# Head dimension first for q and k, contiguous blocks for v and the weights, in a fused attention and mixture kernel

## The chip, the cores and the metric

The kernel runs on one core of one Trainium2 chip. The metric is device time in microseconds (us) of one execution; what the host does to the arrays before the launch is not in it.

## What is computed

A sliding-window attention with sink columns feeds a three-way maximum layer, and that feeds a routed layer of eight experts with a fixed capacity.

```python
scores = (q @ k.T) / sqrt(64)                 # batch 4, heads 8, 768 positions, head dimension 64
keep   = (pos_k < 4) | (0 <= pos_q - pos_k < 128)
a      = softmax(where(keep, scores, -1e9))
x      = (a @ v)                              # to [3072 tokens, 512]
h      = maximum(maximum(x @ w1, x @ w2), x @ w3)       # 512 -> 768
x2     = h @ w_out                            # 768 -> 512
# each token goes to one of 8 experts, 384 each, by the order of all logits x2 @ w_gate
out[t] = relu(x2[t] @ u1[e]) @ u2[e]          # 512 -> 1024 -> 512
```

## The kernel before

**Units and groups.** Attention is cut into 32 units. A unit is one batch, one half of the sequence (`hf`, 384 query rows) and one pair of heads `p`; it reads `nb` = 3 or 4 blocks of 128 key rows. Four units make a group of 384 tokens, and there are 8 groups. A unit goes through `load`, `prep`, `score`, `soft` and `pv`. The first 8 units are "native": their score matmuls take q and k as plain f32. The other 24 split each operand into a high fp32r part and a remainder, and multiply the parts.

**load and prep.** `load` fetches k, q and v with the sequence on the partitions, in rows of 256 B, one DMA for each head (L72, L73, L76), and the sink rows (L74, L77). `prep` (L79) turns them: TensorE transposes each 128x128 block of k and q through `flip` (L25) into the PSUM bank `pt`, of which pool `pst` has one. ScalarE copies out of it, for a native unit into `KZ` and `QF` (L89, L94 for the four sink columns that stand behind each block, L105), for the others into `KH` and `QS` (L89, L94, L114). For these VectorE subtracts to get the remainders (L90, L95, L115), with one operand in PSUM and one in SBUF, and ScalarE copies the high part of k to the other 64 partitions (L118). The unused half of each `KZ` is zero (L56). The native units have two sets of `KZ` in turn (`kf`, in memory lent by `Spare`, which shows as tiles `woh` and `wol`); `early` holds the first k and q loads there too.

**Weights of the first layer.** `single` (L239) loads one 512 KB piece of w1, w2, w3 (rows of 1 KB) or w_out (rows of 4 KB), as float64 words, into `st`, of which there are two buffers, and makes f32 of it on VectorE, ScalarE and GpSimd (L247 to L250). The second L250 of a piece frees its buffer for the next load. `split` makes high and low parts (L237, L238). `group` (L277) is then 216 matmuls of 384 columns for each group (L295), and `x2` 108 more (L317).

**Experts.** For each expert, `weights` (L541) loads 8 pairs `sa` (from u1, rows of 512 B) and `sb` (from u2, rows of 2 KB), two buffers each, splits them on ScalarE, GpSimd and VectorE (L549, L551), and TensorE runs L604 and L597. Between experts VectorE and TensorE choose the next tokens (`Route`).

**What sets the order.** `order` and `order1` (L620) give the order in which units and weight pieces are issued; a scheduler with its own time model then places the instructions on each engine. Each engine and the DMA queue of SyncE (SP) run in that order, so an instruction that waits holds up what is behind it. Tiles in a pool with one buffer (`kn`, `qn`, `vn`) are loaded again when their last reader is done.

Of the kernel before, what the change touches and what calls it, by code (L numbers as in the profile page):

```python
# [22 lines left out]
def f32(ap): return ap.bitcast(FT)  # L23
def flip(nc,out,x,ident):
    nc.tensor.transpose(out,x,f32(ident))  # L25

class Attn:
    def __init__(s, tc, q,k,v, keep, consts, pst, psp, pss, psv, work):
        s.tc=tc; s.nc=nc=tc.nc; s.q,s.k,s.v=q,k,v
# [14 lines left out]
        s.vn=consts.tile([16,2,64],FT,name="vns"); nc.vector.memset(s.vn,0.0)  # L44
# [3 lines left out]
        s.ks=consts.tile([128,2,64],FT,name="kss"); nc.vector.memset(s.ks,0.0)  # L48
# [3 lines left out]
        s.n=0; s.no=('kh0','kh1'); s.early=[]  # L52
# [10 lines left out]
    def load(s,b,hf,p,native=False):  # L63
        nc=s.nc; w=s.w
        nb=3+hf; S=768; D=64
        u=dict(b=b,hf=hf,p=p,nb=nb,n=s.n,nat=native); s.n+=1
        for x,c in (('kn',4),('qn',3)): u[x]=s.early.pop(0) if s.early else w.tile([128,c,2,64],FT,name=x,bufs=1)
        u['vn']=w.tile([128,4,2,64],FT,name="vnn",tag="vsp") if u['nat'] else w.tile([128,4,2,64],FT,name="vn",bufs=1)
        t0=hf*384; tk=t0-128*hf
        def rows(x,h,t,n): return bass.AP(tensor=x.tensor,offset=x.offset+((b*8+2*p+h)*S+t)*D,ap=[[D,128],[128*D,n],[1,D]])  # L70
# [3 lines left out]
        if hf: nc.sync.dma_start(s.ks[0:4],bass.AP(tensor=s.k.tensor,offset=s.k.offset+(b*8+2*p)*S*D,ap=[[D,4],[S*D,2],[1,D]]))  # L74
        for h in range(2):
            nc.sync.dma_start(u['vn'][:,:nb,h,:],rows(s.v,h,tk,nb))  # L76
            nc.sync.dma_start(s.vn[8*h:8*h+8,h],bass.AP(tensor=s.v.tensor,offset=s.v.offset+(b*8+2*p+h)*S*D,ap=[[0,2],[D,4],[1,D]]))  # L77
        return u
    def prep(s,u):  # L79
        nc=s.nc; w=s.w; nb=u['nb']; nat=u['nat']  # L80
        pk=s.pst.tile([128,512],FT,name="pt")
        for c in range(nb):
            flip(nc,pk[:,c*128:(c+1)*128],u['kn'][:,c].rearrange("p h d -> p (h d)"),s.ident)
        def pkv(a): return pk[a,:nb*128].rearrange("p (c j) -> p c j",j=128)
        half=[(slice(64*h,64*h+64),slice(64-64*h,128-64*h)) for h in range(2)]
        KZ=s.kf[u['n']%len(s.kf)] if nat else s.kz[u['n']%len(s.kz)]
        if not nat: KH=[s.two(u,[128,4,132],FR,f"kh{h}") for h in range(2)]
        for h,(a,o) in enumerate(half):
            nc.scalar.activation((KZ if nat else KH)[h][a,:nb,0:128],pkv(a),AF.Copy)  # L89
            if not nat: nc.vector.tensor_tensor(KZ[h][a,:nb,0:128],pkv(a),f32(KH[h][a,:nb,0:128]),op=OP.subtract)  # L90
        def sinks(src):
            for h,(a,o) in enumerate(half):
                ks=src[a][:,None,:].to_broadcast([64,nb-1,4])
                nc.scalar.activation((KZ if nat else KH)[h][a,:nb-1,128:132],ks,AF.Copy)  # L94
                if not nat: nc.vector.tensor_tensor(KZ[h][a,:nb-1,128:132],ks,f32(KH[h][a,:nb-1,128:132]),op=OP.subtract)  # L95
# [4 lines left out]
        if u['hf']:  # L100
            flip(nc,pq[:,384:512],s.ks.rearrange("p h d -> p (h d)"),s.ident)
            sinks(pq[:,384:388])
        if nat:
            QF=w.tile([128,384],FT,name="qf",tag="qs0",bufs=2)
            nc.scalar.activation(QF,pq[:,:384],AF.Copy)  # L105
            u.update(KZ=KZ,QF=QF)
# [62 lines left out]
    def pv(s,u,x):  # L169
# [6 lines left out]
        psk=s.psp.tile([128,512],FT,name="pp")  # L176
# [51 lines left out]
class Moe1:  # L228
    def __init__(s, tc, w1,w2,w3,wout,wgate, consts, wpool, main, conv, mm, pt, pss, ident):
        s.tc=tc; s.nc=tc.nc; s.mm=mm; s.pss=pss; s.main=main; s.conv=conv; s.ident=ident; s.consts=consts  # L230
        s.src=(w1,w2,w3); s.wout=wout; s.wgate=wgate
# [7 lines left out]
    def single(s,src):  # L239
# [506 lines left out]
```

## Time and profile before

| | us |
|---|---|
| three runs: lowest, median, highest | 1033.73, 1038.49, 1040.44 |
| the profiled execution: its own time | 1031.47 |
| its span, first to last instruction | 1029.7 |
| TensorE (PE) busy | 964.8 (94%) |
| VectorE (DVE) busy | 756.8 (73%) |
| ScalarE (ACT) busy | 511.5 (50%) |
| GpSimd (POOL) busy | 409.2 (40%) |

PE busy time counts the pipelined tail of each matmul, so a matmul of 384 columns shows some 340 ns although the next one starts after some 174. The profiled execution was 7.0 us faster than the median of the three runs. It falls into an opening of 100 us, in which attention of the first units and the weights of the first layer are made ready, a long middle to about 625 us with the other units under the matmuls of `group` and `x2`, and the experts.

### The profile page before, as it was taken

The page shows a single profiled execution, that of the slowest core. Times are in us where ns is not written, and L with a number is a line of the kernel's source. Part 1 is how long each engine was busy: PE and PEld are TensorE (multiplying, and loading weights), DVE is VectorE, ACT ScalarE, POOL GpSimd, SP SyncE. Part 2 cuts the span into 40 slices and gives each one's busy share as a digit, 9 for nine tenths or more (in the row PEclk, how much of TensorE's full clock was granted, in tenths as well). Part 3 has the DMA queues.
Part 4 walks back from the last instruction along what each step waited for, and adds up shares of the span by engine and source line. Part 5 has one row for each costly group of instructions (what it writes and reads, how often), then busy time and mean ns, then how long its engine had stood idle before and what let it go on. Part 6 is the DMA issues. An engine that isn't in the chain of part 4 may idle for free.

```text
span 1029.7 us, 19074 instructions
## 1 busy us (share of the span) xinstructions
PE 964.8 (94%) x6857; PEld 878.4 (85%) x6857; DVE 756.8 (73%) x1866; ACT 511.5 (50%) x1166; POOL 409.2 (40%) x355
## 2 busy tenths in 40 slices
PE   5989999999999999999999999898999988999996
PEld 3668889989999999999999998777777877888896
DVE  6799876787988888899886444878888868843330
ACT  5865553676666676665764311332433333344431
POOL 3766636244443434454343100324334243363431
PEclk9899999999999999999999999998999999999999
DMA  6654512132121121121210000424244253464430
GB/s 147 173 150 123 158 43 67 54 98 54 36 57 48 40 78 39 37 66 42 57 42 1 1 1 18 148 88 144 93 134 144 83 165 113 132 197 123 154 102 32
DMA packets 148846, 89.63 MB, mean 87 GB/s; under 512 B 90160, under 2 KB 133680, under 8 KB 148752
## 3 DMA queue, kind: packets, MB, share of 16 engines
q1 hardware_dynamic: 144048, 74.39, 26.0%
q0 software_dynamic: 3840, 12.45, 3.6%
q10 hardware_dynamic: 864, 1.57, 0.4%
q8 instruction: 54, 0.88, 0.3%
q14 instruction: 40, 0.33, 0.1%
HBM read 74.76 MB, written 13.76 MB: 86 GB/s over the span
## 4 chain that ended last, share of the span: by engine, by line
PE 54%; DVE 25%; issue 6%; DMA 6%; ACT 5%; POOL 2%; SPq 0%; POOLq 0%; DVEq 0%; ACTq 0%
PE mm L295 22%; PE mm L604 7%; PE acc L597 7%; PE mm L317 4%; PE po L206 2%; DMA sa<-in_moe_w_dram 2%; PE pt L25 2%; DMA st<-in_moe_w_dram 2%; PE rc L404 2%; DVE th L398 2%; DVE cA L250 2%; DVE A_w L188 1%; PE pp L25 1%; PE ps L142 1%; DVE hl L608 1%
## 5 line engine op out<-in xcount | busy, mean ns | idle before, releaser
L551 POOL TENSOR_TENSOR wal<-sa,wah 128x512 fp32r<-128x512 f32 x64 | 87.4, 1366 | 196.5 <-ACT wah L549 187.0
L202 POOL TENSOR_TENSOR L<-A_w,H 128x768 fp32r<-128x768 f32 x46 | 87.1, 1894 | 141.0 <-ACT H L201 121.8
L317 PE MATMUL mm<-woh,hh 128*128 128x260 f32 (+1 forms) x288 | 84.1, 295 | 2.5 <-DVE LG L320 1.1
L317 PE MATMUL mm<-woh,hl 128*128 128x260 f32 (+1 forms) x288 | 82.8, 292 | 1.9 <-DVE hl L303 1.2
L549 ACT ACTIVATE wah<-sa 128x512 fp32r<-128x512 f32 x64 | 40.4, 631 | 84.4 <-PE mm L604 44.5
L317 PE MATMUL mm<-wol,hh 128*128 128x260 f32 (+1 forms) x288 | 82.3, 287 | 0.0
L298 DVE TENSOR_TENSOR hm<-mm,hm 128x384 f32<-128x384 f32 x96 | 53.0, 552 | 37.6 <-PE mm L295 36.5
L597 PE MATMUL acc<-wbh,hl 128*128 128x512 f32 x192 | 78.5, 409 | 0.2 <-DVE hl L608 0.2
L597 PE MATMUL acc<-wbl,hh 128*128 128x512 f32 x192 | 78.5, 409 | 0.0
L597 PE MATMUL acc<-wbh,hh 128*128 128x512 f32 x192 | 78.2, 407 | 0.0
L549 ACT ACTIVATE wbh<-sb 128x512 fp32r<-128x512 f32 x64 | 40.3, 630 | 75.4 <-PE acc L597 66.5
L608 DVE SCALAR_TENSOR_TENSOR hl<-mm,hh 128x384 fp32r<-128x384 f32 x64 | 35.4, 553 | 56.3 <-ACT hh L607 56.0
L295 PE MATMUL mm<-xh,w0h 128*128 128x384 f32 x192 | 67.3, 351 | 2.0 <-ACT xh L284 1.1
L551 DVE TENSOR_TENSOR wbl<-sb,wbh 128x512 fp32r<-128x512 f32 x64 | 45.6, 714 | 31.5 <-ACT wbh L549 31.0
L295 PE MATMUL mm<-xh,w1h 128*128 128x384 f32 x192 | 66.6, 347 | 2.1 <-DVE hm L298 1.3
L295 PE MATMUL mm<-xl,w0h 128*128 128x384 f32 x192 | 65.6, 342 | 0.8 <-DVE xl L285 0.8
L295 PE MATMUL mm<-xh,w2h 128*128 128x384 f32 x192 | 66.0, 344 | 0.2 <-ACT hm L297 0.2
L295 PE MATMUL mm<-xh,w2l 128*128 128x384 f32 x192 | 65.2, 339 | 0.0
L295 PE MATMUL mm<-xh,w1l 128*128 128x384 f32 x192 | 65.0, 339 | 0.0
L295 PE MATMUL mm<-xl,w2h 128*128 128x384 f32 x192 | 64.8, 338 | 0.0
L295 PE MATMUL mm<-xl,w1h 128*128 128x384 f32 x192 | 64.8, 337 | 0.0
L295 PE MATMUL mm<-xh,w0l 128*128 128x384 f32 x192 | 64.7, 337 | 0.0
(334 smaller groups left out, 3113.4 us busy)
## 6 DMA issues: line engine op xcount, KB each, us to landing
sa<-in_moe_w_dram SPq DMA_DIRECT2D x64, 256.0 KB
sb<-in_moe_w_dram SPq DMA_DIRECT2D x64, 256.0 KB
st<-in_moe_w_dram SPq DMA_DIRECT2D x18, 512.0 KB
qn<-in_q_dram SPq DMA_DIRECT2D x60, 96.0 KB
x2d<-xo SPq DMA_DIRECT2D x18, 256.0 KB
kn<-in_k_dram SPq DMA_DIRECT2D x32, 128.0 KB
st<-in_moe_w_out_dram SPq DMA_DIRECT2D x6, 512.0 KB
vn<-in_v_dram SPq DMA_DIRECT2D x24, 128.0 KB
```

The source lines that it names most:

```text
L25: nc.tensor.transpose(out,x,f32(ident))
L202: nc.gpsimd.tensor_tensor(L,Af,f32(H),op=OP.subtract)
L206: nc.tensor.matmul(po[:,q:q+n],u['VS'][:,blk,128*h:128*h+128],part[:,c:c+n],start=(part is H and j==0),stop=False,skip_group_check=True)
L250: nc.vector.scalar_tensor_tensor(A,st[:,:,1],-0x40000000,A,op0=OP.bitwise_and,op1=OP.bitwise_or)
L295: nc.tensor.matmul(ps[:,:384],s.W[i][a][:,p,f*128:(f+1)*128],X[p][b],start=(n==0),stop=(n==11)); n+=1
L298: else: nc.vector.tensor_tensor(m,ps[:,:384],m,op=OP.max)
L317: nc.tensor.matmul(ps[:,:n],H[f][a][:,t*128:(t+1)*128],s.WO[b][:,f,u,:n],start=(k==0),stop=(k==17)); k+=1
L549: nc.scalar.activation(h,src,AF.Copy)
L551: (nc.vector if s.cv%2==0 else nc.gpsimd).tensor_tensor(l,src,f32(h),op=OP.subtract)
L597: nc.tensor.matmul(acc[t],H[f][a][:,t*128:(t+1)*128],W[f][1][b],start=(f==0 and n==0),stop=(f==F-1 and n==2)); n+=1
L604: nc.tensor.matmul(ps[:,:384],W[f][0][a][:,k,:],X[k][b],start=(n==0),stop=(n==11)); n+=1
L608: nc.vector.scalar_tensor_tensor(l,ps[:,:384],0.0,f32(h),op0=OP.max,op1=OP.subtract)
```

## The change

The host lays the arrays out before the launch. q comes as [128, 384] for each unit: two heads times 64 along the partitions, query rows along the free axis. k comes the same way, with the four sink columns stored behind each block of 128 (132 columns in all). v comes as [128, up to 512], the sink rows of v as one small array `vs`, the words of w1, w2, w3 and w_out as 24 pieces of [128, 4 KB], and u1 in rows of 2 KB. All transposes of k and q go. A native unit's k is loaded right into its half of `KZ`, of which there are now three sets, and its q into `QF`. For the others the ScalarE copies and the VectorE subtractions read `kn` and `qn` in SBUF. `zeros` clears only the unused half of a tile. The transposes of the sink weights in `pv` write to `pst` in place of `psp`.

```diff
     def zeros(s,ts):
-        for t in ts: s.nc.vector.memset(f32(t) if t.dtype==FR else t,0.0)
+        for h,t in enumerate(ts): s.nc.vector.memset((f32(t) if t.dtype==FR else t)[64-64*h:128-64*h],0.0)
...
-        for h in range(2):
-            nc.sync.dma_start(u['kn'][:,:nb,h,:],rows(s.k,h,tk,nb))
-            nc.sync.dma_start(u['qn'][:,:3,h,:],rows(s.q,h,t0,3))
...
+        if native:
+            u['KZ']=s.kf[u['n']%len(s.kf)]
+            for h,(a,o) in enumerate(half): nc.sync.dma_start(u['KZ'][h][a,:nb],turned(h,a))
+            u['QF']=w.tile([128,384],FT,name="qf",tag="qs0",bufs=2)
+            nc.sync.dma_start(u['QF'],s.q[i])
+            u['vn']=w.tile([128,4,2,64],FT,name="vnn",tag="vsp")
+        else:
+            u['kn']=w.tile([128,4,132],FT,name="kn",bufs=1)
+            nc.sync.dma_start(u['kn'][:,:nb],s.k[i].rearrange("h d (c j) -> (h d) c j",j=132)[:,:nb])
+            u['qn']=w.tile([128,384],FT,name="qn",bufs=1)
+            nc.sync.dma_start(u['qn'],s.q[i])
+            u['vn']=w.tile([128,4,2,64],FT,name="vn",bufs=1)
+        nc.sync.dma_start(u['vn'][:,:nb],s.v[i].rearrange("t (c h d) -> t c h d",h=2,d=64)[:,:nb])
+        u['sv']=w.tile([16,2,64],FT,name="vns")
+        nc.sync.dma_start(u['sv'],s.vs[b*4+p].rearrange("r (h d) -> r h d",h=2))
...
-        for c in range(nb):
-            flip(nc,pk[:,c*128:(c+1)*128],u['kn'][:,c].rearrange("p h d -> p (h d)"),s.ident)
...
-            nc.scalar.activation((KZ if nat else KH)[h][a,:nb,0:128],pkv(a),AF.Copy)
-            if not nat: nc.vector.tensor_tensor(KZ[h][a,:nb,0:128],pkv(a),f32(KH[h][a,:nb,0:128]),op=OP.subtract)
...
-        for c in range(3):
-            flip(nc,pq[:,c*128:(c+1)*128],u['qn'][:,c].rearrange("p h d -> p (h d)"),s.ident)
...
             for h,(a,o) in enumerate(half):
-                nc.scalar.activation(QS[h][a,:],pq[a,:384],AF.Copy)
-                nc.vector.tensor_tensor(QS[h][o,:],pq[a,:384],f32(QS[h][a,:]),op=OP.subtract)
-
-                fl=nb*132-4
-                nc.scalar.activation(KH[h][o].rearrange("p c j -> p (c j)")[:,:fl],f32(KH[h][a].rearrange("p c j -> p (c j)")[:,:fl]),AF.Copy)
+                k=flat(u['kn'])[a]
+                for r in (a,o): nc.scalar.activation(flat(KH[h])[r],k,AF.Copy)
+                nc.vector.tensor_tensor(flat(KZ[h])[a],k,f32(flat(KH[h])[a]),op=OP.subtract)
+                nc.scalar.activation(QS[h][a,:],u['qn'][a],AF.Copy)
+                nc.vector.tensor_tensor(QS[h][o,:],u['qn'][a],f32(QS[h][a,:]),op=OP.subtract)
...
-        psk=s.psp.tile([128,512],FT,name="pp")
+        psk=s.pst.tile([128,512],FT,name="pt")
...
-            A.kf=[A.zeros([A.extra.tile([128,4,132],FT,tag=f'kf{i}{h}') for h in range(2)]) for i in range(2)]
-            A.early=[A.extra.tile([128,4,2,64],FT,tag=f'e{i}') for i in range(4)]
+            A.kf=[A.zeros([A.extra.tile([128,4,132],FT,tag=f'kf{i}{h}') for h in range(2)]) for i in range(3)]
...
-        nc.sync.dma_start(a,s.w1[bass.ds(ev,1)].rearrange("a (k p) n -> p (a k) n",p=128)[:,:,f*128:(f+1)*128])
+        nc.sync.dma_start(a,s.w1[bass.ds(ev,1)].rearrange("a (f p) (k n) -> (a f) p k n",p=128,k=4)[f])
...
+def layout(np, i):
...
+    q, k, v = (np.asarray(i[n]).reshape(4, 4, 2, 768, 64) for n in 'qkv')
+    qt = q.transpose(0, 1, 2, 4, 3).reshape(4, 4, 128, 2, 384).transpose(0, 3, 1, 2, 4)
...
+        kt[:, hf, :, :, :, :nb, :128] = k[:, :, :, t].transpose(0, 1, 2, 4, 3).reshape(4, 4, 2, 64, nb, 128)
+        kt[:, hf, :, :, :, :nb, 128:] = k[:, :, :, :4].transpose(0, 1, 2, 4, 3)[:, :, :, :, None, :]
...
+    u1 = np.asarray(i['moe2_w1']).reshape(8, 4, 128, 8, 128).transpose(0, 3, 2, 1, 4)
```

In the changed kernel the lines have moved: L70, L72, L76, L78, L80 and L82 load k (native), q (native), k, q, v and the sinks of v; L99 to L102 are the copies and subtractions of `prep`; L123 are the native score matmuls, L227 the loads of `st`, L276 the matmuls of `group`.

On PE the program begins like this before (`ps<-woh,qf` is a score matmul of a native unit, `pt<-ident` a transpose of its k or q):

```order
L25 MATMUL pt<-ident,woh 128x128 x3
L25 MATMUL pt<-ident,wol 128x128 x3
L139 MATMUL ps<-woh,qf 128x132 x2
L139 MATMUL ps<-woh,qf 128x260
L25 MATMUL pt<-ident,wol 128x128 x3
L139 MATMUL ps<-woh,qf 128x260 x3
L25 MATMUL pt<-ident,wol 128x128 x3
```

and like this with the change, where the score matmuls stand first:

```order
L123 MATMUL ps<-woh,qf 128x132 x2
L123 MATMUL ps<-woh,qf 128x260 x4
L123 MATMUL ps<-woh,qf 128x132 x2
L123 MATMUL ps<-woh,qf 128x260 x4
L123 MATMUL ps<-woh,qf 128x132
L123 MATMUL ps<-wol,qf 128x132
L123 MATMUL ps<-woh,qf 128x260
L123 MATMUL ps<-wol,qf 128x260
```

The transposes ahead of each unit's scores are gone, and three units' scores stand in a row.

On the DMA queue of SP in the opening, before (`kn` and `qn` are loads for the transposes, `vnn` is v, `st` a weight piece):

```order
L263 DMA wg<-in_moe_w_gate_dram 128x4x8
L72 DMA kn<-in_k_dram 128x4x64 x2
L245 DMA st<-in_moe_w_dram 128x4x256
L73 DMA qn<-in_q_dram 128x3x64 x2
L245 DMA st<-in_moe_w_dram 128x4x256
L72 DMA kn<-in_k_dram 128x4x64 x2
L73 DMA qn<-in_q_dram 128x3x64 x2
L74 DMA kss<-in_k_dram 4x2x64
L77 DMA vns<-in_v_dram 8x1x64 x2
L245 DMA st<-in_moe_w_dram 128x4x256
L76 DMA vnn<-in_v_dram 128x3x64 x2
```

and with the change at the same place, where k goes straight into the tiles `woh` and `wol` that the score matmuls of an earlier unit read:

```order
L244 DMA wg<-in_wg_dram 128x4x8
L70 DMA woh<-in_k_dram 64x528
L72 DMA qf<-in_q_dram 128x384
L227 DMA st<-in_words_dram 128x1024
L70 DMA wol<-in_k_dram 64x528
L76 DMA kn<-in_k_dram 128x396
L227 DMA st<-in_words_dram 128x1024
L80 DMA vnn<-in_v_dram 128x384
L227 DMA st<-in_words_dram 128x1024
L70 DMA woh<-in_k_dram 64x528
L72 DMA qf<-in_q_dram 128x384
L70 DMA woh<-in_k_dram 64x528
```

Fewer DMAs are left, and weight pieces now stand behind loads of k and q into tiles that score matmuls release.

On DVE in the middle, around the remainders of one unit with four blocks, before (`kz<-pt,kh` reads PSUM and SBUF):

```order
L90 TENSOR_TENSOR kz_113<-pt,kh_w 64x4x128
L151 COPY_PREDICATED T_w<-ca,ps 128x128
L153 COPY_PREDICATED T_w<-ca,negs 128x8
L175 TENSOR_TENSOR psn<-T_w,psn 128x6x4
L90 TENSOR_TENSOR kz_114<-pt,kh_w 64x4x128
L151 COPY_PREDICATED T_w<-ca,ps 128x128 x2
L157 TENSOR_REDUCE m<-T_w 128x6
L209 TENSOR_TENSOR x_3855<-po,x_3855 64x384
L298 TENSOR_TENSOR hm<-mm,hm 128x384
L163 TENSOR_TENSOR T_w<-T_w,m 128x792
L95 TENSOR_TENSOR kz_113<-pt,kh_w 64x3x4
L298 TENSOR_TENSOR hm<-mm,hm 128x384
```

and with the change, where `kz<-kn,kh` and `qs<-qn,qs` read SBUF twice:

```order
L100 TENSOR_TENSOR kz_109<-kn,kh_w 64x528
L172 TENSOR_TENSOR A_w<-pp,ul 128x768
L135 COPY_PREDICATED T_w<-ca,ps 128x128
L150 TENSOR_SCALAR l<-l 128x6
L102 TENSOR_TENSOR qs_4274<-qn,qs_4274 64x384
L284 TENSOR_TENSOR hl_3178<-hm,hh_3177 128x384
L130 COPY_PREDICATED T_w<-ca,ps 128x128
L131 COPY_PREDICATED T_w<-ca,ps 128x4
L151 RECIPROCAL l<-l 128x6
L100 TENSOR_TENSOR kz_110<-kn,kh_w 64x528
L135 COPY_PREDICATED T_w<-ca,ps 128x128
L102 TENSOR_TENSOR qs_4275<-qn,qs_4275 64x384
```

The two small sink subtractions are gone, and those of k and q stay, with another source.

## Rows read from the trace of the kernel before

**Rows 1.** Busy time of each engine by stretch: from:to in us, length, then each engine.

```profile
0.00:100.00 100.00, 82.28 (x423) 63.24 (x424) 84.65 (x180) 65.72 (x189) 59.75 (x62) 0.97 0.57 151
100.00:150.00 50.00, 47.47 (x290) 41.79 (x291) 42.51 (x82) 29.35 (x68) 24.61 (x23) 1.00 0.36 104
150.00:600.00 450.00, 440.55 (x3032) 430.81 (x3031) 362.32 (x759) 271.04 (x629) 182.01 (x156) 1.00 0.18 47
650.00:900.00 250.00, 224.97 (x2055) 189.37 (x2054) 204.13 (x692) 87.80 (x171) 93.61 (x73) 0.97 0.40 125
```

**Rows 2.** Chain that ended last, 0 to 150 us: start, length, what.

```profile
3.75 0.51 DVE woh L56
4.29 0.89 PE pt L25 x3
5.20 0.48 ACT woh L89
...
6.63 0.91 PE pt L25 x3
7.57 0.50 ACT qf L105
8.11 2.11 PE ps L139 x6
...
83.86 3.76 DMA st<-in_moe_w_dram
...
147.53 0.33 PE pt L25 x3
```

**Rows 3.** The same chain's later pieces, 150 us to the end.

```profile
175.94 3.72 DMA st<-in_moe_w_out_dram
...
751.11 4.65 DMA sa<-in_moe_w_dram
...
827.84 7.53 DMA sa<-in_moe_w_dram
```

**Rows 4.** Who waited for whom on DVE, 0 to 50 us: total, times, longest.

```profile
DVE T_w L151 <- ACT T_w L150: 5.1, 5, 1.7
DVE T_w L146 <- PE ps L139: 3.1, 1, 3.1
```

**Rows 5.** Transposes by tile kn, qn, kss in 150 to 600 us: PE, then PEld.

```profile
150.00:600.00 450.00, 12.30 (x75) 9.36 (x75) 1.00 0.18 47
150.00:600.00 450.00, 10.50 (x63) 7.88 (x63) 1.00 0.18 47
150.00:600.00 450.00, 3.27 (x12) 1.69 (x12) 0.00 (x0) 1.00 0.18 47
```

**Rows 6.** VectorE by line: shortest, median, longest ns. L115, L298 read PSUM; L303 SBUF twice.

```profile
L115 DVE TENSOR_TENSOR qs<-pt,qs x48: 550/555/560, 86.8 to 539.4; 64x384 fp32r<-64x384 f32 x48
L298 DVE TENSOR_TENSOR hm<-mm,hm x96: 536/557/562, 72.9 to 623.8; 128x384 f32<-128x384 f32 x96
L303 DVE TENSOR_TENSOR hl<-hm,hh x48: 516/558/2101, 81.1 to 625.0; 128x384 fp32r<-128x384 f32 x48
```

**Rows 7.** Groups by form: count, then busy us and mean ns of one.

```profile
L303 DVE TENSOR_TENSOR hl<-hm,hh 128x384 fp32r<-128x384 f32 x48 | 36.0, 750 | 7.7 <-ACT hh L302 7.3
L298 DVE TENSOR_TENSOR hm<-mm,hm 128x384 f32<-128x384 f32 x96 | 53.0, 552 | 37.6 <-PE mm L295 36.5
```

**Rows 8.** The removed ScalarE copies and VectorE sink subtractions, by line: shortest, median, longest ns.

```profile
L89 ACT ACTIVATE woh<-pt x16: 483/534/595, 5.2 to 58.9; 64x384 f32<-64x384 f32 x8, 64x512 f32<-64x512 f32 x8
L94 ACT ACTIVATE woh<-pt x16: 158/172/176, 6.2 to 61.9; 64x8 f32<-64x8 f32 x8, 64x12 f32<-64x12 f32 x8
L105 ACT ACTIVATE qf<-pt x8: 472/490/490, 7.6 to 62.1; 128x384 f32<-128x384 f32 x8
L95 DVE TENSOR_TENSOR kz<-pt,kh_w x26: 114/164/177, 75.3 to 517.0; 64x8 fp32r<-64x8 f32 x14, 64x12 fp32r<-64x12 f32 x12
```

**Rows 9.** What the SP queue waited for: total, times, longest.

```profile
SPq L72 <- PE ps L143: 67.1, 13, 10.4
SPq L72 <- PE pt L25: 52.2, 11, 10.9
```

More of the change, by code (lines that the diff above doesn't have):

```diff
@@ L27, with __init__ @@
 class Attn:
-    def __init__(s, tc, q,k,v, keep, consts, pst, psp, pss, psv, work):
-        s.tc=tc; s.nc=nc=tc.nc; s.q,s.k,s.v=q,k,v
+    def __init__(s, tc, q,k,v,vs, keep, consts, pst, psp, pss, psv, work):
+        s.tc=tc; s.nc=nc=tc.nc; s.q,s.k,s.v,s.vs=q,k,v,vs
         s.pst,s.psp,s.pss,s.psv,s.w=pst,psp,pss,psv,work
@@ L43, in __init__ @@
         s.ps=consts.tile([128,160],FR,name="psn"); nc.vector.memset(f32(s.ps),0.0)
-        s.vn=consts.tile([16,2,64],FT,name="vns"); nc.vector.memset(s.vn,0.0)
         s.vk=[]
@@ L47, in __init__ @@
             t=consts.tile([128,2,128],FR,name=f"vk{i}"); nc.vector.memset(f32(t),0.0); s.vk.append(t)
-        s.ks=consts.tile([128,2,64],FT,name="kss"); nc.vector.memset(s.ks,0.0)
         s.kf=[]; s.kz=[s.zeros([consts.tile([128,4,132],FR,name=f"kz{h}") for h in range(2)])]
@@ L51, in __init__ @@
         nc.scalar.activation(t,t,AF.Exp)
-        s.n=0; s.no=('kh0','kh1'); s.early=[]
+        s.n=0; s.no=('kh0','kh1')
         s.extra=None
@@ L66, in load, with turned @@
         u=dict(b=b,hf=hf,p=p,nb=nb,n=s.n,nat=native); s.n+=1
[L67 to L70, printed above, removed]
-        for h in range(2):
-            nc.sync.dma_start(u['kn'][:,:nb,h,:],rows(s.k,h,tk,nb))
-            nc.sync.dma_start(u['qn'][:,:3,h,:],rows(s.q,h,t0,3))
[L74 to L77, printed above, removed]
+        i=(b*2+hf)*4+p; c=nb*132; half=[(slice(64*h,64*h+64),slice(64-64*h,128-64*h)) for h in range(2)]
+        def turned(h,a): return s.k[i,h].rearrange("d (c j) -> d c j",j=132)[:,:nb]
+        if native:
[13 more added lines that the diff above has]
+        nc.sync.dma_start(u['sv'],s.vs[b*4+p].rearrange("r (h d) -> r h d",h=2))
         return u
@@ L80, in prep @@
         nc=s.nc; w=s.w; nb=u['nb']; nat=u['nat']
-        pk=s.pst.tile([128,512],FT,name="pt")
-        for c in range(nb):
-            flip(nc,pk[:,c*128:(c+1)*128],u['kn'][:,c].rearrange("p h d -> p (h d)"),s.ident)
-        def pkv(a): return pk[a,:nb*128].rearrange("p (c j) -> p c j",j=128)
         half=[(slice(64*h,64*h+64),slice(64-64*h,128-64*h)) for h in range(2)]
-        KZ=s.kf[u['n']%len(s.kf)] if nat else s.kz[u['n']%len(s.kz)]
-        if not nat: KH=[s.two(u,[128,4,132],FR,f"kh{h}") for h in range(2)]
@@ L88, in prep @@
-        for h,(a,o) in enumerate(half):
-            nc.scalar.activation((KZ if nat else KH)[h][a,:nb,0:128],pkv(a),AF.Copy)
-            if not nat: nc.vector.tensor_tensor(KZ[h][a,:nb,0:128],pkv(a),f32(KH[h][a,:nb,0:128]),op=OP.subtract)
[L91 to L95, printed above, removed]
@@ L96, in prep @@
-        if not u['hf']: sinks(pk[:,0:4])
-        pq=s.pst.tile([128,512],FT,name="pt")
-        for c in range(3):
-            flip(nc,pq[:,c*128:(c+1)*128],u['qn'][:,c].rearrange("p h d -> p (h d)"),s.ident)
[L100 to L106, printed above, removed]
@@ L107, in prep @@
         VK=u['VK']=s.vk[u['n']%2]
         hi,lo=(bass.AP(tensor=VK.tensor,offset=VK.offset+o,ap=[[VK.ap[0][0],16],[st,2],[1,64]]) for o,st in (((0,64),(128,64)) if nat else ((0,192),(64,64))))
-        nc.gpsimd.tensor_copy(hi,s.vn)
-        nc.gpsimd.tensor_tensor(lo,s.vn,f32(hi),op=OP.subtract)
+        nc.gpsimd.tensor_copy(hi,u['sv'])
+        nc.gpsimd.tensor_tensor(lo,u['sv'],f32(hi),op=OP.subtract)
         if not nat:
+            KZ=s.kz[u['n']%len(s.kz)]
+            KH=[s.two(u,[128,4,132],FR,f"kh{h}") for h in range(2)]
@@ L618, in expert, with attention_mixtures @@
             s.scat.append(st)
-def attention_mixtures(tc,q,k,v,w1,w2,w3,wo,wg,u1,u2,out,off=236,native=8,order='a0 a0 a0 a0 w a1 a1 w w w w w a1 a1 a2',order1='a2 o o o o o o a2 a2',acc='011100000010',back=1,at=(1,0),s1=300,s2=400,nring=6):
+def attention_mixtures(tc,q,k,v,vs,words,wg,u1,u2,out,off=236,native=8,order='a0 a0 a0 a0 w a1 a1 w w w w w a1 a1 a2',order1='a2 o o o o o o a2 a2',acc='011100000010',back=1,at=(1,0),s1=300,s2=400,nring=6):
     nc=tc.nc
@@ L630, in attention_mixtures @@
         x2d=dram.tile([3072,512],FT,name="x2d")
-        A=Attn(tc,q,k,v,consts,ac,pst,psp,pss,psv,work)
-        M=Moe1(tc,w1,w2,w3,wo,wg,consts,wpool,main,conv,mm,pst,pss,A.ident)
+        A=Attn(tc,q,k,v,vs,consts,ac,pst,psp,pss,psv,work)
+        M=Moe1(tc,words,wg,consts,wpool,main,conv,mm,pst,pss,A.ident)
         M.at=at
@@ L732 @@
     arrays, args = {}, []
+    laid = layout(_np, inputs)
     for name in _INS:
-        a = _np.ascontiguousarray(inputs[name])
-        if a.dtype == _np.float64:
-            a = a.view(_np.int64)
+        a = _np.ascontiguousarray(laid[name])
         arrays[f"in_{name}_dram"] = a
```

30 lines of the change are left out of this document (21 added, 9 removed).

## The prediction

> **What bounds the kernel now.** I read the stretches first, then the chain that ended last, then the waits. In the stretches [rows 1] the reader is to see three regimes. From 0 to 100 us PE has gaps (82.28 busy) and so has DVE (84.65); from 150 to 600 us PE is busy 440.55 of 450 us, DVE 362.32 and ACT 271.04; from 650 to 900 us PE is busy 224.97 of 250. The chain says what the gaps are made of. The opening is a string of steps of one unit after another: transposes on PE, copies on ACT, score matmuls, and loads of weight pieces of some 3.7 us [rows 2]. In the middle the chain is mostly PE's own matmuls, which is what a nearly full PE means: work taken from PE there is time, work taken from the others is time only where PE waits for them.
>
> **The opening.** Before, PE starts its first transposes at 4.29 us, when the loads are there and the first `KZ` half is cleared, then ACT copies, PE turns q, ACT copies q, and the first scores run at 8.11 us [rows 2]. The change leaves the loads and the clearing. Both halves of a set have to be cleared, so one more memset of 0.51 us may count: first scores between 4.3 and 4.9 us, I take 4.6, which gives 3.5 us. Behind it ACT loses, for the 8 native units, 16 copies of 0.534, 16 of 0.172 and 8 of 0.490 us [rows 8], 15.2 us of the 65.72 that it works in the first 100 us [rows 1]. ACT is not the bound there; what counts is that DVE waited 5.1 us in the first 50 for ACT's score copies, which stand behind those copies in ACT's order [rows 4]. I take half of that, 2.5 us. Together 6.0 us. The ends: 2 us, if the loads of the second and third unit land too late for the earlier start, and 10 us, if all of the 5.1 and most of DVE's other gaps go (15.35 us in 100, of which 3.1 is the first wait that the 3.5 us already hold).
>
> **The transposes in the middle.** Three transposes of one tile take 0.33 us on the chain [rows 2], so 0.11 us each; the 270 ns and more that one shows as busy are pipelined. From 150 to 600 us there are 75 for k, 63 for q and 12 for the sinks [rows 5], 150 in all. 150 times 0.11 is 16.5 us of PE. Those of the first 150 us are not counted, since PE has gaps there. How much of the 16.5 becomes time: PE's gaps of 9.45 us in the 450 [rows 1] stay, and now and then PE comes earlier to a step of DVE or ACT that is not earlier, and waits. The upper end is 16.5, the lower 10, an estimate as if four in ten transposes had stood beside such a step. I take the middle, 13.3 us.
>
> **ACT and DVE in the other 24 units.** ACT does the same number of long copies: two of the high part of k in place of one from PSUM and one from SBUF, and loses the small sink copies. I cost it at nothing, hidden under PE; ACT is busy 271.04 of 450 us [rows 1]. DVE loses 48 sink subtractions of 0.164 us [rows 8], 7.9 us. Its 96 subtractions for k and q stay, but read SBUF twice in place of PSUM and SBUF. L115, from PSUM, takes 550 to 560 ns and never more, L298 at most 562; L303, the same width from SBUF twice, has a median of 558 but a longest of 2101 [rows 6] and a mean of 750 against 552 [rows 7]. So each moved subtraction costs between nothing (median to median) and 198 ns (mean to mean), 0 to 19.0 us in all. L303 runs in the same stretch beside the same GpSimd work, so I take its mean: 19.0 less 7.9, 11.1 us more for DVE. That makes 373 us of DVE work in about 436, 86%: still under PE, so nothing on the path; its ends are 0 and the whole 11.1.
>
> [...]
>
> **Memory traffic.** Packets grow, but loads need not be faster. A 512 KB weight piece with rows of 1 KB lies 3.76 us on the chain [rows 2], one of w_out with rows of 4 KB 3.72 us [rows 3]. So the pieces of w1, w2, w3, which get rows of 4 KB, gain nothing: 0. Of the experts' loads, those of u1 (rows of 512 B) lie 4.65 and 7.53 us on the chain, where a burst of four loads starts after the routing [rows 3]. Rows of 2 KB may shorten them, but PE is idle only 25.0 us in the whole stretch [rows 1], and much of it falls to routing. I take 2 us, 0 and 8 as ends; the nearest row, the weight pieces, speaks for the lower half.
>
> [...]
>
> **The rest.** Moving the sink weights' transposes to the idle bank of `pst` takes a wait off `psp` in every unit; none of it is seen on PE's stretch, and I cost it at nothing, with 1 us to either side. The clearing of a third `KZ` set is two memsets of 0.51 us [rows 2] off the first unit's path, since they are not its own set. The added wait is on the DMA queue: a native k now waits until the score matmuls three units earlier have read `KZ`. Behind it in SP's order stand weight pieces (the order shows it at three places, and seven in the whole opening). Before, k waited for transposes and for scores there too: 52.2 us for transposes and 67.1 us for scores over the run [rows 9]. With three sets in place of two I cost it at nothing; what it costs if the cover is gone is the second rival.
>
> **Sum.** 6.0 + 13.3 + 2 = 21.3 us. The profiled execution took 1031.47 us, so it would take 1010.2. The runs shown have a median 7.0 us above it, and I forecast on their scale: 1038.5 less 21.3 gives 1017.2, predicted as 1017. The ends: 10 + 16.5 + 8 + 1 = 35.5 less gives 1003; 2 + 10 less 1 for `pst` is 11 less, 1027.5.
>
> **Rivals.** First, DVE becomes the bound of the middle. [...] Then the 11.1 us of DVE work stands against the 13.3 of PE, and what is left is 6.0 + 2 + 2.2 = 10.2 us, or with the lower ends of the opening and the experts 2 + 0 + 2.2 = 4.2: 1028 to 1034. Against: PE hardly waited for DVE there, and DVE has 87.7 us of slack in 450 [rows 1].
>
> Second, slower: the weight pieces get stuck behind native k loads on SP's queue. One wait of SP for scores is 67.1/13 = 5.2 us [rows 9]. If all seven pieces behind such loads came late by this, 36 us would be added to the opening and the total would be 1038.5 - 21.3 + 36 = 1053. It decides from five pieces on, since 4.1 times 5.2 us eat the gain. Against: a piece has two buffers, and scores now come earlier than before.
>
> Third, the 256 B rows were a brake on the opening, where the DMA engines are 57% busy [rows 1]: then each of the five weight pieces on the opening's chain ([rows 2] hold one of them) lands earlier by an estimated 1 to 2 us, as if its 3.76 were cut by half at most, and the time is 1017 - 10 = 1007 or, with the upper ends of the other terms, under 1002. Against: 3.76 and 3.72.
>
> Fourth, the scheduler places the rest worse by as much as the transposes were worth, so that the change does not give what it takes away: 6.0 + 2 less 0 to 13.3 us of new waits, 1030 to 1044.
>
> **Chances.** The forecast, 1002 to 1028: 0.72 (with the third rival's milder half). DVE as the bound: 0.11. SP's queue, slower by over 1%: 0.05. Under 1002 (third with upper ends): 0.06. Placement: 0.06. A change of 1%, 10.4 us, is about what a measurement of this kernel can tell from no change. So faster by over 1%: 0.78; within 1%: 0.16; slower: 0.06. The range must leave out no more than 2 in 10; from 1002 to 1030 holds the forecast's cases and the better part of the first rival's.
>
> **What would show it.** The first scores at 4 to 5 us; the last matmuls of `group` some 17 to 22 us earlier than before; the stretch with the 24 units shorter by 10 to 17 us at the same PE share; L100 and L102 with medians near 0.56 us and longest over 1 us; weight pieces still 3.7 us on the chain. I am wrong if DVE is above 92% busy in the middle with PE under 95%, if SP's waits ahead of L227 grow, or if the loads of `st` or `sa` fall by more than 1 us and the opening ends over 12 us earlier.

## The result and the profile after

The changed kernel takes 1052.17 us (four runs, 1050.73 to 1054.88), the kernel before 1036.99 beside it (1033.73 to 1040.44). The ratio is 1.0149, with an interval of 1.0107 to 1.0191: 15 us slower, where 21 us faster was forecast. The profiled execution took 1051.36 us with a span of 1049.6. The profiled execution of the kernel before (1031.47) was over 5 us faster than the runs here, so the two profiles lie 20 us apart where the runs lie 15.

The stretches of the changed kernel, as in [rows 1]:

```profile
0.00:100.00 100.00, 77.77 (x378) 59.51 (x379) 91.30 (x180) 53.61 (x151) 61.36 (x62) 0.95 0.49 149
150.00:600.00 450.00, 416.69 (x2773) 407.04 (x2773) 343.34 (x687) 258.75 (x573) 181.25 (x153) 0.97 0.15 47
650.00:900.00 250.00, 225.63 (x2154) 191.71 (x2152) 197.80 (x670) 84.31 (x166) 88.12 (x69) 0.96 0.38 122
```

PE is busy 24 us less from 150 to 600 us. That is more than the transposes' 16.5, so it is no gain: PE stands idle 33.3 us there, against 9.45 before. To see where, I count the progress of the group work. For 200 to 330 us the next fence gives all engines, then PE's instructions of `group` and then of `x2` alone; first the kernel before (L295, L317):

```profile
200.00:330.00 130.00, 126.49 (x890) 123.05 (x888) 111.38 (x228) 87.41 (x209) 53.93 (x48) 0.99 0.23 60
200.00:330.00 130.00, 59.14 (x300) 0.99 0.23 60
200.00:330.00 130.00, 38.60 (x261) 0.99 0.23 60
```

and the changed kernel (L276, L298):

```profile
200.00:330.00 130.00, 110.90 (x734) 106.09 (x735) 118.14 (x227) 89.67 (x199) 64.66 (x52) 0.92 0.21 62
200.00:330.00 130.00, 42.67 (x216) 0.92 0.21 62
200.00:330.00 130.00, 34.17 (x211) 0.92 0.21 62
```

In these 130 us the changed kernel does 134 group matmuls less (216 + 211 against 300 + 261), and DVE is busy 91% of the time. The last remainder of `group` (L284) starts at 643.1 us, where L303 did at 625.0 [rows 6], and at the end the lag is 20 us. The waits of PE from 200 to 330 us say for what:

```profile
PE ps L126 <- DVE T_w L135: 5.8, 4, 3.8
PE mm L298 <- DVE LG L301: 3.8, 2, 3.2
PE mm L298 <- DVE hl L315: 2.2, 2, 1.2
```

Score matmuls (`ps`) wait for DVE to clear the PSUM banks of the scores ahead of them, and the group matmuls stand behind them in PE's order. Beside some of these waits stands a second loss. Around a wait of 3.2 us that ended at 203.0, two of 1.25 us from 225.5 on and one of 3.8 us from 314.9 on, TensorE's granted clock fell, at 203.4, 227.3 and 316.0, from 1.00 to 0.50 (lines of PE alone):

```profile
203.40:206.80 3.40, 3.40 (x18) 0.50 0.45 135
206.80:210.20 3.40, 3.40 (x31) 1.00 0.00 0
227.30:234.10 6.80, 5.59 (x24) 0.50 0.37 131
316.00:326.30 10.30, 6.12 (x26) 0.50 0.31 91
```

In 3.4 us without a gap PE ran 18 instructions at 0.50 and 31 at 1.00. By that, the 15.1 us that it was busy at 0.50 cost some 6 us (an estimate). That the waits bring the falls on is not shown: waits of 1.9 us up to 214.1 and of 1.5 us up to 268.6 had none beside them, and before, where no wait in the stretch took 1 us, the clock still fell once, for 3.4 us from 213.0 on (0.51 in the mean).

Later the picture turns: the last subtraction of q starts at 491.7 us (539.4 before, [rows 6]), and from there PE finishes the group work with DVE ever less busy.

Why DVE is that crowded from 200 to 330 us can be counted in the order of the two programs: how many group matmuls stand in PE's stream ahead of the first score matmul of a unit (units counted from 0, four to a group):

| | units 12 to 15 | 16 to 19 | 20 to 23 |
|---|---|---|---|
| before | 562 657 708 776 | 862 936 1008 1068 | 1151 1224 1320 1392 |
| after | 468 539 568 612 | 684 759 798 840 | 898 972 1020 1080 |
| blocks only, and v alone (experiments below) | 540 597 682 744 | 804 869 936 1008 | 1080 1152 1224 1308 |
| the other 24 turned (an experiment below) | 488 540 564 613 | 696 768 813 868 | 936 1008 1081 1128 |
| paced (an experiment below) | 496 540 684 731 | 864 899 1016 1049 | 1188 1224 1344 1373 |

A group has 324 matmuls and takes four units, so one per 81 would be even. Before, a unit comes every 75 group matmuls; after, one comes every 55: the scheduler writes the units further and further ahead of the group that will use them. In the experiments it is 70 with v, sinks and weights in blocks and the transposes still there, and 58 once the 24 units' transposes go as well.

### The profile page after: what moved, and what is told of

It reads as the page before. It is cut to its first block, busy times and chain, and to the rows that moved or that the text cites. A ratio compares the mean times of both kernels' runs of the same rounds, so it can differ in the third digit from the quotient of the medians.

```text
span 1049.6 us, 18421 instructions
## 1 busy us (share of the span) xinstructions
PE 952.8 (91%) x6633; PEld 866.2 (83%) x6633; DVE 757.7 (72%) x1818; ACT 492.3 (47%) x1078; POOL 414.7 (40%) x355
## 4 chain that ended last, share of the span: by engine, by line
PE 52%; DVE 27%; issue 8%; ACT 6%; DMA 3%; POOL 1%; SPq 1%; POOLq 0%; another core or an unknown queue 0%; ACTq 0%; DVEq 0%
PE mm L276 19%; PE mm L585 7%; PE mm L298 7%; PE acc L578 7%; PE po L190 3%; PE rc L385 2%; DVE qs L102 2%; DVE th L379 2%; DVE cA L232 1%; DVE m L141 1%; DVE A_w L172 1%; DVE psn L159 1%; DVE hl L284 1%; PE pp L25 1%; DVE wbl L532 1%
## 5 line engine op out<-in xcount | busy, mean ns | idle before, releaser
L532 POOL TENSOR_TENSOR wal<-sa,wah 128x512 fp32r<-128x512 f32 x64 | 87.9, 1373 | 196.9 <-ACT wah L530 189.4
L298 PE MATMUL mm<-woh,hh 128*128 128x260 f32 (+1 forms) x288 | 86.7, 302 | 6.5 <-DVE LG L301 3.8
L298 PE MATMUL mm<-woh,hl 128*128 128x260 f32 (+1 forms) x288 | 84.2, 297 | 3.0 <-DVE hl L315 2.2
L298 PE MATMUL mm<-wol,hh 128*128 128x260 f32 (+1 forms) x288 | 84.3, 294 | 0.0
L276 PE MATMUL mm<-xh,w1h 128*128 128x384 f32 x192 | 66.1, 344 | 3.7 <-DVE hm L279 2.7
L276 PE MATMUL mm<-xh,w0h 128*128 128x384 f32 x192 | 66.7, 347 | 1.8 <-DVE hm L279 1.7
L276 PE MATMUL mm<-xh,w2h 128*128 128x384 f32 x192 | 66.6, 347 | 0.4 <-ACT hm L278 0.4
L276 PE MATMUL mm<-xl,w0h 128*128 128x384 f32 x192 | 65.6, 342 | 0.6 <-DVE xl L266 0.6
L276 PE MATMUL mm<-xl,w2h 128*128 128x384 f32 x192 | 65.5, 341 | 0.0
L276 PE MATMUL mm<-xh,w2l 128*128 128x384 f32 x192 | 65.2, 339 | 0.0
L276 PE MATMUL mm<-xh,w1l 128*128 128x384 f32 x192 | 65.1, 339 | 0.0
L276 PE MATMUL mm<-xl,w1h 128*128 128x384 f32 x192 | 64.9, 338 | 0.0
L276 PE MATMUL mm<-xh,w0l 128*128 128x384 f32 x192 | 64.8, 337 | 0.0
```

The costliest lines, as they stand in the source:

```text
L276: nc.tensor.matmul(ps[:,:384],s.W[i][a][:,p,f*128:(f+1)*128],X[p][b],start=(n==0),stop=(n==11)); n+=1
L298: nc.tensor.matmul(ps[:,:n],H[f][a][:,t*128:(t+1)*128],s.WO[b][:,f,u,:n],start=(k==0),stop=(k==17)); k+=1
L532: (nc.vector if s.cv%2==0 else nc.gpsimd).tensor_tensor(l,src,f32(h),op=OP.subtract)
```

## The experiments

The theories, as the expectations name them. 1, pace: the transposes that went were what spaced the units out, and without them the units crowd the streams. 2: the subtractions on VectorE, now with two SBUF operands, make VectorE the bound. 3: the bank of the sink weights' transposes (`pst` for `psp`) makes PE wait. 4: block loads, or their place in SP's queue. 5: what the scheduler makes of a small difference in loads costs the time. Each kernel was timed in five rounds beside the kernel before; ratios are to it.

**Halves of the change.** v, sinks and weights are in blocks in all; the units' q and k come turned for none, the native ones, or the other 24. The first three have the bank of before. (There are eight native units; the text on record says four.)

```diff
+NATNEW,RESTNEW=False,False    # e2: True,False   e3: False,True
...
-        if native:
+        new=NATNEW if native else RESTNEW
+        if new and native:
```

> v, the sinks, the words and the expert's first weights come in blocks, as in the changed kernel; q and k of all 28 units are still loaded as they lie and transposed on TensorE. Theory 1 (pace): the transposes that went were what spaced the attention units out between the group matmuls, and without them the scheduler writes the units ahead of the group work, so VectorE is full early and TensorE waits. Here the transposes stand, so the time is that of the kernel before, 1032 to 1040 us. Theory 2 (the subtractions of the split on VectorE read two SBUF operands and take longer, and VectorE is the bound): the old subtractions stand here too, so also 1032 to 1040 us. Theory 4 (the block loads themselves, or their place in SyncE's queue, cost the time): 1045 to 1055 us here.

> As the run with blocks only, but the four native units take q and k with the head dimension first: their transposes and copies go, the other 24 units keep theirs. The order of the units among the group matmuls is that of the kernel before. Theory 1 (pace): the opening is lighter and nothing behind it moves ahead, 1028 to 1037 us. Theory 2 (subtractions on VectorE): only units without a split lose anything, so no subtraction changes, and the time is also 1028 to 1037 us. Theory 4 (native loads in SyncE's queue): 1043 to 1055 us here.

> The other half: the 24 units with split q and k take them with the head dimension first, the four native ones are transposed as before. Units stand as far ahead of the group matmuls as in the changed kernel. Theory 1 (pace): 1047 to 1056 us, with VectorE over 85% busy and TensorE under 90% from 200 to 400 us. Theory 2 (subtractions): the same time, with 9 to 11 us more of subtractions on VectorE. Theory 4 (native loads): that of the kernel before, 1032 to 1040 us.

The fourth is the whole change but for the bank:

```diff
-        psk=s.pst.tile([128,512],FT,name="pt")
+        psk=s.psp.tile([128,512],FT,name="pp")
```

> The changed kernel with one thing undone: the transposed probabilities of the split units have their PSUM bank in the pool that they had before, not in that of the transposes. Theory 3 (the waits on that bank of the transposes cost the time): back to 1035 to 1042 us. Theories 1 and 2: 1047 to 1056 us, no different from the changed kernel by more than 4 us.

Measured: blocks only gave 1052.4 us, 1.0144 (1.0104 to 1.0184); native units turned as well 1051.07, 1.0147; the other 24 turned 1061.73, 1.0253 (1.0214 to 1.0292); all, with the bank of before, 1064.95, 1.0278. The last two lie above every range given. Three things follow. The native units' turned loads cost and bring nothing. Theory 3 has its sign wrong: the move to the other bank is worth 13 us in favour of the change. And blocks alone, without an operation of q or k touched, already cost 15 us, which only theories 4 and 5 allow; theory 1 said 1032 to 1040 us there, so it can be a part at most. Its part shows in the next step: from blocks only to the other 24 turned the time rises by 9 us, although PE loses the transposes of these units, and the pace goes from 70 to 58.

**Weights alone, v alone.** The blocks taken apart, on the kernel before. Weights:

```diff
-            x=s.src[i].bitcast(I32).rearrange("(k p) n -> p k n",p=128)[:,:,f*256:(f+1)*256]
+            v=s.single(s.src[f*3+i]).rearrange("p (k n) -> p k n",k=4)
```

> The kernel before with only the words of the first mixture's weights and the expert's first weights in blocks, and the half memsets; q, k, v and the sinks as before. TensorE, ScalarE and GpSimd run word for word the instructions of before in its order. Theory 5 (what cost 15 us in the run with blocks only is the place that the scheduler gave the units once v and sinks came in fewer loads): 1030 to 1037 us here. Theory 4 (the block loads of the weights themselves cost it): 1045 to 1055 us here.

v and sinks:

```diff
-            nc.sync.dma_start(u['vn'][:,:nb,h,:],rows(s.v,h,tk,nb))
+        nc.sync.dma_start(u['vn'][:,:nb],s.v[i].rearrange("t (c h d) -> t c h d",h=2,d=64)[:,:nb])
```

> The kernel before with v and the sinks alone in blocks: one load of v for two and one of the sinks for two or three, no operation of any engine added or gone. The scheduler places the units then as in the run with blocks only. Theory 5 (that order is what cost 15 us there): 1045 to 1055 us. If the block loads of the weights were part of it, 1035 to 1043 us.

Measured: weights 1035.98 us, 1.0000 (0.9976 to 1.0024); v 1047.94 us, 1.0132 (1.0097 to 1.0167). So the weights' blocks are worth nothing either way, with the order unchanged, and theory 4 falls for them. The blocks of v and the sinks cost nearly all of the 15 us, and but for one clearing of a small tile that goes they neither add nor take away work on any engine. What differs is the loads and, with them, the order, from the opening on. PE's group matmuls from 0 to 100 us (L295) in the kernel before:

```profile
0.00:100.00 100.00, 25.16 (x120) 0.97 0.57 151
```

and with v's blocks:

```profile
0.00:100.00 100.00, 23.33 (x103) 0.95 0.56 156
```

The fifth unit's scores stand ahead of the first group matmuls there (0 ahead of it, 6 before). The opening holds only part of the loss. From 200 to 330 us v's blocks give these group and `x2` matmuls (L295, L317):

```profile
200.00:330.00 130.00, 46.83 (x236) 0.97 0.23 63
200.00:330.00 130.00, 45.69 (x301) 0.97 0.23 63
```

They are 17 matmuls behind the kernel before at 100 us, 37 at 200 (460 against 497) and 61 at 330 (997 against 1058). Whether the order or the loads themselves make the loss, the run of v alone doesn't tell apart; the first paced run below has the same loads and is faster than the kernel before, so the loads don't have to cost it.

**Order alone.** One number of the scheduler changed in the kernel before:

```diff
-def attention_mixtures(...,off=236,
+def attention_mixtures(...,off=100,
```

> The kernel before with one number changed, the lead that the scheduler gives the attention units over the group work (100 for 236): the same instructions and loads, 668 of TensorE's rows moved in the order of its stream, the opening untouched. Theory 5 (an order alone is worth 10 us and more): outside 1030 to 1042 us, by at least 5 us. Theory 2 (VectorE is the bound by what it has to do): 1030 to 1042 us.

Measured: 1042.74 us, 1.0055 (1.0031 to 1.0079). The same instructions in another order, 5.7 us more. An order alone does cost time, though less than theory 5 said. Its units 12 to 23 stand 77 matmuls apart, no closer than before, so the pace isn't all that an order does.

**The change with an even pace.** q of the split units is loaded into the ring of `group`'s tile `hm`, so that a unit's load waits until the group has come to a certain place; the places are the second kernel's only difference. In the first the units come in pairs, one unit for every 80 group matmuls in the mean.

```diff
-            u['qn']=w.tile([128,384],FT,name="qn",bufs=1)
+            u['qn']=s.qpool.tile([128,384],FT,name="qn",tag="hm",bufs=2)
...
+        HOOK,HP=['x', 'x', (0, 0), (1, 2)],True    # e8: ['x', 'x', 'x', (2, 0)]
...
+                if hook is not None: hook(f,i)
```

> The changed kernel, with the units paced again: q of the split units is loaded into the ring of the group's product tiles, so a unit's load waits for the group to reach a place (two units behind a group's first half, two behind steps of the next). No operation is added. Units stand some 50 to 100 group matmuls apart, as in the kernel before, in place of 40 to 60 in clusters. Theory 1 (pace): the loss between 200 and 330 us goes, 1030 to 1040 us. Theory 2 (the subtractions on VectorE): 1045 to 1056 us, since every one of them stands.

> As the run before, with three units behind a group's first half and one in the next, so the pace is less even: 1032 to 1043 us by theory 1, 1045 to 1056 us by theory 2.

Measured: 1032.47 us, 0.9950 (0.9927 to 0.9972), and 1040.49 us, 1.0041 (1.0021 to 1.0060). Every operation of the change stands, the subtractions too, and 20 us of it are gone: at the changed kernel's loads and operations the pace is worth that much, and theory 2 falls as the main cause. The less even pace gives 8 of them back. With the ring q also has two buffers in place of one; no run takes that apart from the pace, but the less even kernel has the ring too. The first paced kernel, 200 to 330 us, as above (L276, L299):

```profile
200.00:330.00 130.00, 119.18 (x804) 114.64 (x803) 104.41 (x199) 81.87 (x181) 56.66 (x48) 0.97 0.20 58
200.00:330.00 130.00, 57.47 (x300) 0.97 0.20 58
200.00:330.00 130.00, 36.36 (x236) 0.97 0.20 58
```

300 group matmuls again, as before, and DVE at 80%.

**Less work on VectorE.** k's subtractions on GpSimd in the changed kernel, then k's and q's in turn in the first paced one:

```diff
-                nc.vector.tensor_tensor(flat(KZ[h])[a],k,f32(flat(KH[h])[a]),op=OP.subtract)
+                nc.gpsimd.tensor_tensor(flat(KZ[h])[a],k,f32(flat(KH[h])[a]),op=OP.subtract)
```

```diff
-                nc.vector.tensor_tensor(QS[h][o,:],u['qn'][a],f32(QS[h][a,:]),op=OP.subtract)
+                nc.gpsimd.tensor_tensor(QS[h][o,:],u['qn'][a],f32(QS[h][a,:]),op=OP.subtract)
```

> The changed kernel with k's 48 subtractions of the split on GpSimd in place of VectorE: 41 us of VectorE's work go (48 of 720 to 914 ns), at the changed kernel's crowded order, whose units stay 40 to 60 group matmuls apart. Theory 1 (the order alone): the units still crowd 200 to 330 us, 1043 to 1055 us. Theory 2 (VectorE's load is what the crowd runs into): 1030 to 1042 us. Both can be part of one cause: then it lies between, and the run shows how much VectorE's load is of it.

> The first paced run with k's subtractions on GpSimd. If VectorE's load still costs time where the pace is even (it is 81% busy there from 150 to 600 us, TensorE 95%), this gives 3 to 10 us, 1022 to 1030 us. If TensorE waits for steps in sequence and not for VectorE's capacity, 1030 to 1036 us, and slower if GpSimd's steps, longer than VectorE's, come to stand in the chain of a unit.

> The first paced run with q's subtractions on GpSimd: 32 us of VectorE's work go. As for k's: 1023 to 1030 us if VectorE's capacity still costs, 1030 to 1036 us if not.

Measured: 1058.71 us, 1.0230 (1.0196 to 1.0265); 1036.60, 1.0006; 1028.33, 0.9931 (0.9901 to 0.9962). At the crowded order the relief makes it slower by 6 us, outside both theories' ranges. Its q subtractions, still on DVE, say why it is no plain relief (count, busy us and mean ns). The changed kernel:

```profile
L102 DVE TENSOR_TENSOR qs<-qn,qs 64x384 fp32r<-64x384 f32 x48 | 34.5, 720 | 3.9 <-ACT qs L101 2.4
```

and this one:

```profile
L102 DVE TENSOR_TENSOR qs<-qn,qs 64x384 fp32r<-64x384 f32 x48 | 50.8, 1059 | 14.2 <-ACT qs L101 12.4
```

By the trace of the changed kernel k's subtractions are 39.0 us, not the 41 of the expectation. Of these, 16 come back in the 48 instructions above alone, beside a busier GpSimd (470.1 us against 414.7), and DVE's busy time falls from 757.7 to 749.1 us only. The order moved too, by up to 111 group matmuls towards the crowd (the unit at 759 stands at 648), so how much of the 6 us is which stays open. At the paced order, which moves by no more than 29, k on GpSimd costs 4 us against the paced run, as its expectation allowed, and q on GpSimd lands in the range given for VectorE's capacity. The run with q on GpSimd is the fastest version found that keeps all of the work; its interval overlaps the paced run's, so only its lead over the kernel before is certain.

To see VectorE's part without that, k's subtractions are left out (and the tiles that they wrote are cleared in whole):

```diff
-                nc.vector.tensor_tensor(flat(KZ[h])[a],k,f32(flat(KH[h])[a]),op=OP.subtract)
```

> The first paced run with k's subtractions left out (the second part of k's split is zero, so the scores lose it): 41 us of VectorE's work go and nothing takes its place on another engine. If VectorE's steps are what TensorE's idle time from 150 to 600 us comes from, 5 to 15 us shorter than the paced run, 1017 to 1027 us. If not, within 3 us of it.

Measured: 1024.08 us, 0.9896 (0.9871 to 0.9921), 8 us below the paced run. VectorE's steps do cost time, about a fifth of their busy time (38.5 us in the paced kernel).

**The transposes put back as dead weight**, in the first paced kernel, the changed kernel and the kernel before:

```diff
+        for i in range(0 if u['nat'] else u['nb']+3): flip(nc,psk[:,384:512],f32(s.ident),s.ident)
         for i in range(3): nc.tensor.transpose(psk[:,i*128:(i+1)*128].bitcast(FR),PS[:,16*i:16*i+128],s.ident)
```

> The first paced run with TensorE's transposes put back as dead weight: each split unit transposes the identity 6 or 7 times into columns of the probabilities' PSUM tile that nobody reads, 156 transposes of 0.11 us, about 17 us of TensorE. Order and pace stay as in the paced run within 20 matmuls. If the prediction's term for the transposes holds at an even pace (they are on the path from 150 to 600 us), 13 to 17 us longer than the paced run, 1044 to 1050 us. If TensorE has that time free anyway, because it waits for the units' steps, within 3 us of the paced run, 1030 to 1036 us.

> The changed kernel, in its crowded order, with the 156 dead transposes of the paced dummy run. There they cost 20 us for 17 us of TensorE. If at the crowded order TensorE has that time free from 200 to 330 us, where it waits for the units, less than half: 1052 to 1060 us. If their time is on the path here too, 1066 to 1074 us, and the order's cost and the transposes' gain simply add.

> The kernel before with the same 156 dead transposes on top of its own, 17 us of TensorE. Its order shifts with them by up to 90 matmuls towards the crowd in the later groups. If TensorE bounds the stretch from 150 to 600 us, as the prediction said, 13 to 20 us, 1049 to 1057 us; if it has time free there, 1036 to 1044 us.

Measured: 1052.65 us, 1.0158 (1.0124 to 1.0192); 1063.53 us, 1.0266 (1.0240 to 1.0292); 1054.69 us, 1.0180 (1.0155 to 1.0205). They are there as meant, by the view of the tile (shortest, median, longest ns, then first and last start), in the paced kernel:

```profile
L25 PE MATMUL pt<-ident x156: 270/273/333, 118.9 to 581.4; 128*128 128x128 f32 x156
```

156 times 0.11 us is 17 us, and they cost 20, 11 and 18.5 us. In the paced kernel the units stay within 16 group matmuls of their places, so there the transposes' time on PE is time, and the run lies above its range for that. In the other two kernels the dead transposes moved the order as well, units by up to 75 and 98 matmuls towards the crowd, so the 11 and the 18.5 us hold both and aren't the price of the transposes alone. The middle run lies between its two expectations.

**The bank once more, and another pace.** The paced kernel with `psk` in `psp` (diff above), and q on GpSimd with the places of the third group's units spread out:

```diff
-        HOOK,HP=['x', 'x', (0, 0), (1, 2)],True
+        PTS,HP=[[], [(5, 2)], [(0, 2), (1, 2), (2, 2), (5, 2), (5, 2)], [(0, 0), (1, 2), (5, 2), (5, 2)], ...],True
```

> The first paced run with the transposed probabilities in their PSUM bank of before. At the crowded order that undoing cost 12 us. If the bank itself is worth that (a step waits for it), 1042 to 1048 us here too. If it was the order that came with it, 1030 to 1038 us; the opening's order comes out changed here as well, so part of it, up to 8 us before 130 us, may stay.

> q's subtractions on GpSimd, with the third group's units given out at five even places, so that the units stand nearer to the pace of the kernel before from 200 to 300 us. If pace is what is left there, 1 to 5 us below the paced run with q's subtractions on GpSimd: 1023 to 1028 us; if not, 1028 to 1033 us.

Measured: 1056.54 us, 1.0206 (1.0176 to 1.0237), and 1034.53, 1.0006 (0.9982 to 1.0030). Both missed. The first is 24 us above the paced run, and most of it is lost in the opening. Group matmuls (L276) from 0 to 100 us in the paced kernel:

```profile
0.00:100.00 100.00, 27.79 (x132) 0.93 0.48 150
```

and in this one:

```profile
0.00:100.00 100.00, 17.16 (x82) 0.88 0.48 147
```

With the bank go both waits (the transposes into `pp` waited 4.8 us for ACT in the first 150 us here) and the opening's order, as the native units' scores then stand at other places among the group matmuls; which of the two costs it stays open. The second, 6 us above the run with the same subtractions and the first places, says that a spacing nearer to that of before in one group is not enough to go by.

## Why the prediction was wrong

The transposes' gain was there. The prediction gave 13.3 us, at most 16.5, for 150 transposes in the middle; 156 put back cost 20 us at the paced order, where they left the order as it was. What failed is that the sum priced each edit in the streams as they stood, with a new order at nothing, and let the order change in one rival only: "the scheduler places the rest worse by as much as the transposes were worth", with a chance of 0.06. The mechanism of that rival is the one that happened in the middle: pacing the units, with every operation of the change left in, gave 20 us back. But its bound had no ground. Nothing ties the cost of a worse order to the work that left. If the 11 us by which the dead transposes slowed the changed kernel are taken as their gain there, it lost 15 + 11, about 26 us (an estimate, since they moved the order), where the rival allowed at most 13.3. About 14 us come already with v and the sinks alone, an edit that the prediction did not price at all.

Step by step:

- First scores: 4.95 us, after a forecast of 4.6 and at most 4.9.

```profile
4.95 2.09 PE L123 MATMUL ps<-woh,qf 128*128 128x132 f32 x6 [4.95 <-DMA qf<-in_q_dram]
```

  Of that lead little stayed: 12 group matmuls at 100 us (132 against 120) and 7 at 200 us (504 against 497), 2 and 1 us at 174 ns each, an estimate. The term of 6.0 came out near nothing. DVE's wait for ACT's score copies in the first 50 us did fall, from the 5.1 of [rows 4]:

```profile
DVE T_w L135 <- ACT T_w L134: 2.3, 3, 1.2
```

  Yet DVE was then busy 91.3 of the first 100 us, after 84.65. That it had no room for what came earlier is likely, and no run shows it.
- DVE's subtractions got dearer as forecast: 720 ns in the mean for q's, where 750 was taken from [rows 7], with a shortest of 551. All 96 took 73.5 us against 56.2, so 17.3 more, where 19.0 was taken. On the path the prediction had 0 to 11.1 us for 11.1 us more of DVE work. By the fifth that leaving k's out gave, it is about 2 us, an estimate. With k's on GpSimd they got dearer still: the same 48 subtractions of q took 720 ns in the mean with GpSimd busy 414.7 us, in the changed kernel, and 1059 with it busy 470.1 us, in that run; what makes them dearer is not shown.
- The first rival, DVE as the bound of the middle, holds for 200 to 330 us alone. It is a consequence of the order there: at an even pace DVE is at 80%.
- The second, SP's queue: SP did wait longer ahead of the weight pieces (51.8 us in 15 waits against 36.8 in 9), which the prediction named as a sign against it.

```profile
SPq L245 <- DVE cA L250: 36.8, 9, 15.8
SPq L227 <- DVE cA L232: 51.8, 15, 11.9
```

  But the native units' turned loads, which put those loads ahead of the pieces, changed nothing (1.0144 without, 1.0147 with). The sign was no proof.
- Weights' pieces at 0 was right (1.0000). That run left q, k and v in rows of 256 B, so it says nothing of the third rival. In the changed kernel, without those rows, two pieces are left on the opening's chain, at 4.99 and 3.31 us, and the opening wasn't 10 us shorter for it; no run shows the 1 to 2 us that the rival took for each piece:

```profile
12.89 4.99 DMA st<-in_words_dram
98.86 3.31 DMA st<-in_words_dram
```

- The experts' loads were sized at 2 us and came out at nothing: the run with weights alone had their new rows too, `sa` still lies on the chain, and the stretch takes PE 225.63 us, as before (224.97).

```profile
769.66 4.04 DMA sa<-in_u_dram
...
885.05 5.30 DMA sa<-in_u_dram
```

- The move to the idle bank, priced at 0 with 1 us to either side, came out at 13 us at the crowded order and 24 at the paced one, in favour of the change, with whatever order came along with it.

What stays open: whether the 14 us of v's blocks come from the order or from the loads, and why; and whether the bank works by its wait or by the order. At an even pace the whole change brings 4 us, and 8 with q's subtractions on GpSimd, not the 18 that the dead transposes cost in the kernel before. The rest may lie in the order of before, which no paced kernel reached: there PE was busy 440.55 of 450 us, in the first paced kernel 428.74. No run shows it, nor how such an order is found.

## What to carry to other kernels

Where a scheduler writes the order, an edit has two prices, that of its own operations and that of the new order, and the second can be the larger; even an edit that only merges loads can bring another order. Before forecasting, count in the built program how far each producer stands ahead of its consumer along the bound engine's stream, for the whole of it and not for three places: a pace of 55 where the kernel before has 75 was there to be read without a run. If a removed step was what held producers back, put another hold in its place, here a shared ring of buffers, before judging the edit.

## What was unexpected on the chip

- Work moved from VectorE to GpSimd came back in part: with k's subtractions on GpSimd, VectorE's 48 subtractions of q rose from 34.5 to 50.8 us, and of the 39.0 us that left VectorE its busy time fell by 8.6.
- From 200 to 330 us the granted clock was 0.92 in the mean in the changed kernel and 0.99 before. It stood at 0.50 for 3.4, 6.8 and 10.3 us, some 16% of that stretch, and before for 3.4 us. PE had waited there for up to 3.8 us at a time; before, no wait in the stretch took 1 us. By the estimate in the section on the result, the time at 0.50 cost some 6 us beyond the waits themselves; that the waits bring it on is not shown.
